# Attention and a gated feed-forward on one core: first batch's sums by a product with ones, weights summed as integers

## The chip, the cores and the metric

The kernel runs on one core of a Trainium2 chip. The metric is the device time of one execution in microseconds. Three runs of the kernel before took 865.38, 866.71 and 871.32 us; their median is 866.71 us. The engines are named as in the profile: PE multiplies matrices, PEld is its loading of weights, DVE is the vector engine, ACT the scalar engine, POOL is GpSimd, and SP issues most transfers. L502 is line 502 of the kernel before.

## The reference

The reference computes attention with a threshold, for 8 batches of 8 heads with 576 tokens of 64 numbers, and then a feed-forward over the 4608 rows of 512 numbers that come out of it.

```python
scores = scale * np.matmul(q, k.transpose(0, 1, 3, 2))
thresh = np.max(scores, axis=-1, keepdims=True) - tau
scores = np.where(scores >= thresh, scores, -1000000000.0)
scores = scores - np.max(scores, axis=-1, keepdims=True)
attn = np.exp(scores)
attn = attn / (np.sum(attn, axis=-1, keepdims=True) + 1e-09)
attn_out = np.matmul(attn, v)
# the heads of a token side by side: x is 4608 x 512
h = x @ w_in
e = np.exp(h - np.max(h, axis=-1, keepdims=True))
solu = h * (e / (np.sum(e, axis=-1, keepdims=True) + 1e-09))
mu, var = mean and variance of solu over its 1024 columns
ln = (solu - mu) / np.sqrt(var + 1e-06) * g_ln
out = ln @ w_out
```

`q`, `k` and `v` are 32-bit floats. [...]

## The kernel before, in words

**Slots and rounds.** The attention is cut into 144 slots, 18 for each batch. A slot is 128 query rows of two heads (`hp` is the pair of heads). Slots of kind 0 and 1 hold the first 512 tokens of a pair of heads in four parts; the two slots of kind 2 hold what is left of all eight heads. Two slots, r = 0 and r = 1, form a unit. The main loop runs in rounds, one slot in each, and writes out by hand the order of the work on every engine; nothing is reordered afterwards. "pv(10)" below is the product pv that round 10 issues, and likewise "scores(11)".

**What a round does**, by engine, in the order of issue:

- PE: `scores` (L480) into two PSUM tiles `s0` and `s1`, one for each head of the slot. There is one buffer for each, so the next round's scores wait until ACT has read this round's. Then a part of the feed-forward (`ff_h`, L655, in two halves h0 and h1 of 32 matmul records; `ff_o`, L760), and, where a unit is due, `attend_steps`: the product pv (L590), 72 matmul records. A unit is due three or four rounds after its second slot: pv runs in rounds 5, 7, 9, 10, 12, 15, 16 and 19 for the eight units of the first batch. PE works strictly in this order, so scores(r+1) stand behind pv(r).
- DVE: `maxes` (L502) takes the largest score of each row, for two heads. Then `blocks` (L548) transposes the slot of the round before in 32 x 32 blocks into the tile `T`, with an instruction for each head; at r = 1 three transfers on SP's queue bring `T` into the tile `wT` (L557, L559), which pv reads. Then come the weights, and in later rounds the reductions of the feed-forward (L670, L685, L700).
- ACT: `ramp` (L517) and `exps` (L526) make the weights of attention from the scores; `exps` also sums each row into `sm`, which shows in the profile as an extra instruction that reads the accumulator. `attended` copies the product from PSUM to `xh` (L622), the input of the feed-forward.
- POOL: `normalise` of the slot of the round before: add 1e-9 to the sums (L533), their inverse by a power (L534), and a product for each head (L536).

**The weights.** In rounds 0 to 15 each round also turns one of 16 pieces of the weights (128 x 512 numbers, 512 KB) into floats. Pieces 0 to 7 are `w_in`, 8 to 15 are `w_out`. `weight_load` brings a piece into `raw`. `weight_a` cuts exponent (L286 on DVE, L291 on ACT) and the mantissa's upper part (L292 on DVE) out of the upper word. `weight_b` adds the lower word to the mantissa (L306) and the sign to the exponent (L309), both on DVE with two inputs. `weight_c` multiplies the two on POOL (L319), a round later and behind that round's `normalise`. For `w_out` ACT also multiplies the exponent part by the gains (`weight_gain`, L325), and `weight_d` (L332) makes a copy with the halves of the partitions swapped, by transfers on SP's queue.

**Buffers.** Two PSUM tiles (`p0`, `p1`, handed out in turn by `take`) hold the products pv, `h_ps` and `o_ps`; a tile of pv is free after the copy L622. In rounds 0, 2 and 4 `whole_pair` uses both to transpose the q and k of a pair of heads (L345 on PE, copied out by ACT). `T` and `wT` have two buffers each; `e` of a weight piece has two, its `m` one. From round 13 on PE also transposes q and k of the second batch (L345 again), which needs their transfers (`load_one`, `load_ends`, L131 and L142).

Of the kernel before, what the change touches and what calls it, by code (L numbers as in the profile page):

```python
# [20 lines left out]
def kernel(  # L21
# [61 lines left out]
    lims = [const.tile([P, 1], F32, name=f"lim{x}") for x in range(2)]  # L83

    wide = w_in.dtype == I64
    W_UNIT = 2.0**-20 if wide else 1.0
# [159 lines left out]
    def gains():  # L246
        tag, g_ps = take("g_ps")
        nc.tensor.transpose(out=g_ps[:, 0:NC], in_=g_rows, identity=ident[0:NC, 0:NC])
        nc.vector.tensor_scalar(
            out=gs, in0=g_ps[:, 0:NC], scalar1=W_UNIT, scalar2=None, op0=ALU.mult  # L250
        )
        pairs_free.append(tag)
# [5 lines left out]
    def piece(x):  # L258
        if x < 2 * NP:
            c, hf = divmod(x, 2)  # L260
            cols = slice(512 * hf, 512 * hf + 512)
            return w_in[P * c : P * c + P, cols], w1[:, c, cols], W_UNIT
        c = x - 2 * NP
        return w_out[P * c : P * c + P], w2[:, 2 * c], gs[:, c : c + 1]
# [12 lines left out]

    def weight_a(x):
        if not wide:
            return  # L280
        d = raws[x]
        hi = d["raw"].bitcast(I32).rearrange("p (n two) -> p n two", two=2)[:, :, 1]
# [8 lines left out]
        nc.scalar.activation(out=e, in_=e, func=AF.Relu, bias=lims[x >= 2 * NP], scale=8388608.0)  # L291
        nc.vector.tensor_scalar(  # L292
            out=m, in0=hi, scalar1=0xFFFFF, scalar2=0x100000,
            op0=ALU.bitwise_and, op1=ALU.bitwise_or,
        )

    def weight_b(x):
        d = raws[x]
        _, dst, unit = piece(x)
        if not wide:  # L300
            nc.vector.tensor_scalar(out=dst, in0=d["raw"], scalar1=unit, scalar2=None, op0=ALU.mult)
            return
        words = d["raw"].bitcast(I32).rearrange("p (n two) -> p n two", two=2)
        lo, hi = words[:, :, 0], words[:, :, 1]
        e, m = d["em"]
        nc.vector.scalar_tensor_tensor(  # L306
            out=dst, in0=lo.bitcast(U32), scalar=2.0**-32, in1=m, op0=ALU.mult, op1=ALU.add
        )
# [4 lines left out]
    def weight_c(x):  # L313
        d = raws.pop(x)
        if not wide:
            return
        _, dst, _ = piece(x)
        e, _ = d["em"]
        nc.gpsimd.tensor_tensor(out=dst, in0=dst, in1=e.bitcast(F32), op=ALU.mult)  # L319
# [136 lines left out]
    live = {}  # L456

# [33 lines left out]
    def maxes(s, loose):  # L491
# [3 lines left out]
        both = small.tile([P, 2], F32, tag="both", name="both") if loose else None  # L495
        for ps in d["ps"]:
# [4 lines left out]
            w = work.tile([P, S], F32, tag="w", bufs=4, name="w")  # L501
# [19 lines left out]

    def exps(s):
        d = live[s]
        d["sm"] = sm = small.tile([P, 2], F32, tag="sm", name="sm")
# [5 lines left out]
    def normalise(s):  # L530
        d = live[s]
        sm = d["sm"]
# [7 lines left out]
    def blocks(s):  # L540
# [6 lines left out]
        for h, w in enumerate(live.pop(s)["w"]):  # L547
# [20 lines left out]
    def attend_steps(key):  # L568
# [7 lines left out]
        for e in range(2) if kind == 2 else [None]:  # L576
            for m in range(NK):
                for u in range(2):
                    d, h0 = source(b * NP + (hp if e is None else e + 2 * u))
                    for h in range(2):  # L580
# [18 lines left out]
                        yield  # L599

    def attended(key):
        b, kind, hp = key
        tag, y = units.pop(key)["y"]
        y = y.rearrange("p (u n) -> p u n", u=2)[:, :, 0:P]
        if kind == 2 or b < 2:
            y = y.rearrange("p u (r y) -> p u r y", r=2)
        else:
# [7 lines left out]
        else:  # L615
# [252 lines left out]
    with tc.manual_schedule():  # L868
# [29 lines left out]
        while True:  # L898
# [29 lines left out]
            if rnd - 1 in pieces:  # L928
                weight_gain(pieces[rnd - 1])
# [113 lines left out]
            if rnd in pieces:  # L1043
# [46 lines left out]
```

## Time and profile before

| what | value |
|---|---|
| three runs | 865.38, 866.71, 871.32 us |
| span of the profiled execution | 865.3 us |
| PE busy, over the span | 820.6 us (95%) |
| DVE, ACT, POOL busy | 682.6, 574.2, 500.2 us (79%, 66%, 58%) |
| rounds 0 to 18 (first batch and one) | begin at 10.9 us, round 19 at 118.8 us |
| DVE busy, 20 to 90 us | 67.3 of 70 us |
| PE busy, 20 to 90 us | 49.1 of 70 us |
| PE busy, 200 to 800 us | 596.8 of 600 us |

The page gives the span of the profiled execution, from its first instruction to its last, and no time of its own; the fastest run, 865.38 us, is 0.1 us longer than that span, the median 1.4 us.

A round's begin is the begin of its first L502 on DVE. In order they are (us): 10.9, 16.1, 21.4, 26.8, 31.5, 36.7, 41.4, 46.6, 51.3, 56.5, 61.2, 67.0, 71.5, 78.6, 85.1, 91.9, 100.3, 106.7, 111.1 and 118.8.

How to read the views: a line of the timeline has the start, the length in us, the engine, the line of the kernel, the operation, the tiles (out<-in), the shapes, how many instructions are merged, and in square brackets the idle time of the engine before it and what ended it. A matmul in 32-bit floats leaves two records, so a count of 72 is 36 matmul instructions. "PEclk" is the clock granted to PE, as a share of full speed.

### The profile page before, as it was taken

The numbers are of one execution on the slowest core, as the hardware profiler recorded it, in microseconds if no ns is written. First come the engines' busy times: TensorE is split into PE (matmuls) and PEld (weight loads), VectorE is DVE, ScalarE is ACT, GpSimd is POOL, SyncE is SP. The second block draws the span as 40 slices with busy tenths as digits, with TensorE's granted clock in tenths as the row PEclk, the third lists the DMA queues.
The fourth block names the chain that finished last, engine by engine and source line by source line (L and its number), as shares of the span: only waits on it lengthen the run. The fifth ranks groups of instructions, "written<-read, shape, count | busy, mean of one in ns | idle before, by whom it ended". The sixth has DMA issues, their size and how long they took to land.

```text
span 865.3 us, 36120 instructions
## 1 busy us (share of the span) xinstructions
PE 820.6 (95%) x15361; PEld 633.6 (73%) x15361; DVE 682.6 (79%) x1248; ACT 574.2 (66%) x1153; POOL 500.2 (58%) x938
## 2 busy tenths in 40 slices
PE   5667999899999999999999999999999999999997
PEld 3444667677688887777777776777799998887655
DVE  4999778878788888888788887888888888787361
ACT  5887767767767767677677776777677776775121
POOL 2888656556656656565656655565666655555120
PEclk9788899999999999999999999999999999999999
DMA  8999787988878788988878877887788877655212
GB/s 256 273 261 238 192 190 176 229 237 203 222 188 232 200 191 197 225 221 191 212 190 223 204 188 186 220 221 203 190 224 229 205 180 189 154 142 139 69 38 62
DMA packets 83712, 168.54 MB, mean 195 GB/s; under 512 B 15448, under 2 KB 45152, under 8 KB 83552
## 3 DMA queue, kind: packets, MB, share of 16 engines
q1 hardware_dynamic: 82416, 164.25, 76.2%
q8 instruction: 120, 1.97, 1.0%
q10 hardware_dynamic: 1136, 2.00, 0.7%
q14 instruction: 40, 0.33, 0.1%
HBM read 46.14 MB, written 9.44 MB: 64 GB/s over the span
## 4 chain that ended last, share of the span: by engine, by line
PE 81%; DMA 7%; ACT 4%; DVE 2%; SPq 2%; issue 2%; POOL 1%; ACTq 0%; DVEq 0%
PE o_ps L760 26%; PE h_ps L655 22%; PE s_ps L480 15%; PE pv L590 15%; PE h_ps L645 3%; DMA wT<-T 3%; ACT w L517 1%; ACT w L526 1%; DMA ends<-in_q_dram 1%; DVE w L502 1%; DMA w<-w 1%; DMA qT<-flip 1%; DMA k<-in_k_dram 1%; DVE T L548 1%; POOL w L536 1%
## 5 line engine op out<-in xcount | busy, mean ns | idle before, releaser
L760 PE MATMUL o_ps<-w,uT 64*64 64x256 f32 x4608 | 274.3, 376 | 2.4 <-DMA w<-w 1.3
L502 DVE CUSTOM_DVE_ANT_0 w<-s_ps,tau_t 128x576 f32<-128x576 f32 x280 | 200.3, 753 | 87.5 <-PE s_ps L480 57.5
L517 ACT ACTIVATE w<-s_ps,nth 128x576 f32<-128x576 f32 x280 | 197.0, 739 | 104.9 <-DVE nth L502 94.1
L760 PEld LDWEIGHTS o_ps<-w,uT 64*64 64x64 f32 x4608 | 215.3, 133 | 62.8 <-ACT xh L622 11.0
L536 POOL TENSOR_SCALAR w<-w,sm 128x576 f32<-128x576 f32 x288 | 222.2, 784 | 14.3
L655 PE MATMUL h_ps<-w,xh 64*64 64x512 f32 x1856 | 225.3, 592 | 1.1 <-issue 1.1
L548 DVE STREAM_TRANSPOSE T<-w 128x576 f32<-128x576 f32 x288 | 207.6, 755 | 19.8 <-POOL w L536 19.4
L526 ACT ACTIVATE w<-w,ntau 128x576 f32<-128x576 f32 x288 | 219.6, 767 | 0.0
L590 PEld LDWEIGHTS pv<-wT,v 64*64 64x64 f32 x5760 | 179.0, 136 | 32.4 <-issue 8.5
L480 PE MATMUL s_ps<-kT,qT 64*64 64x64 f32 (+1 forms) x2048 | 183.2, 422 | 14.0 <-ACT w L517 12.1
L590 PE MATMUL pv<-wT,v 64*64 64x128 f32 (+1 forms) x5760 | 177.7, 264 | 7.4 <-DMA wT<-T 4.7
L655 PEld LDWEIGHTS h_ps<-w,xh 64*64 64x64 f32 x1856 | 134.8, 134 | 65.4 <-issue 15.6
L533 POOL TENSOR_SCALAR sm<-sm 128x2 f32<-128x2 f32 x144 | 36.5, 253 | 202.0 <-ACT w L526 198.9
L534 POOL TENSOR_TENSOR sm<-sm,mone 128x2 f32<-128x2 f32 x144 | 109.0, 757 | 12.0
L480 PEld LDWEIGHTS s_ps<-kT,qT 64*64 64x64 f32 x2048 | 78.3, 139 | 23.4 <-ACT w L517 17.3
L622 ACT COPY xh<-pv 128x256 f32<-128x256 f32 x64 | 25.2, 394 | 81.3 <-PE pv L590 81.3
L721 ACT ACTIVATE V<-u,nb,rs 128x1024 f32<-128x1024 f32 x36 | 44.7, 1241 | 38.8 <-POOL nb L711 31.8
L747 DVE STREAM_TRANSPOSE uT<-V 128x1024 f32<-128x1024 f32 x36 | 44.2, 1226 | 16.9 <-DMA V<-u 16.8
L526 ACT ACTIVATION_READ_ACCUMULATOR w<-w,ntau 128x1 f32 x288 | 55.5, 193 | 0.0
L685 DVE TENSOR_TENSOR u<-h_ps,u 128x1024 f32<-128x1024 f32 x36 | 42.8, 1189 | 9.8 <-ACT u L679 9.8
L726 DVE TENSOR_SCALAR u<-u,rs,nb 128x1024 f32<-128x1024 f32 x36 | 35.0, 973 | 17.8 <-ACT V L721 17.7
L670 DVE TENSOR_REDUCE hm<-h_ps 128x1 f32<-128x1024 f32 x36 | 42.9, 1193 | 5.4 <-PE h_ps L645 2.7
(90 smaller groups left out, 578.0 us busy)
## 6 DMA issues: line engine op xcount, KB each, us to landing
wT<-T SPq DMA_DIRECT2D x160, 288.0 KB, 6.3
wT<-T SPq DMA_DIRECT2D x64, 576.0 KB, 5.6
V<-u SPq DMA_DIRECT2D x144, 64.0 KB, 3.4
out_dram<-ob SPq DMA_DIRECT2D x71, 128.0 KB, 2.5
q<-in_q_dram SPq DMA_DIRECT2D x24, 288.0 KB, 6.2
qT<-flip SPq DMA_DIRECT2D x48, 144.0 KB, 3.5
k<-in_k_dram SPq DMA_DIRECT2D x24, 288.0 KB, 6.4
kT<-flip SPq DMA_DIRECT2D x48, 144.0 KB, 3.8
```

The lines of the kernel that those rows point to most:

```text
L480: nc.tensor.matmul(out=ps[h][ROWS[y], ks], lhsT=lhsT, rhs=d["kT"][ROWS[h], ks], start=True, stop=True,)
L502: nc.vector.tensor_tensor_reduce(out=w, in0=ps[:, 0:S], in1=(zero if loose else tau_t).to_broadcast([P, S]), scale=1.0, scalar=BIG, op0=AL ...
L517: nc.scalar.activation(out=d["w"][x], in_=d["w"][x] if d["loose"] else d["ps"][x][:, 0:S], func=AF.Prelu, bias=d["nth"][x], scale=-1.0, al ...
L526: nc.scalar.activation(out=w, in_=w, func=AF.Exp, bias=ntau, scale=1.0, accum_out=sm[:, x : x + 1])
L534: nc.gpsimd.tensor_tensor(out=sm, in0=sm, in1=mone, op=ALU.pow)
L536: nc.gpsimd.tensor_scalar(out=w, in0=w, scalar1=sm[:, x : x + 1], scalar2=1.0, op0=ALU.mult, op1=ALU.mult)
L548: nc.vector.transpose(out=T[:, :, r, h, :], in_=w)
L590: nc.tensor.matmul(out=to, lhsT=d["v"][ROWS[u], (h0 + h - u) % 4 if b > 1 else h0 + h, m ^ 4 * u if m < 8 and b < 2 else m,], rhs=rhs, sta ...
L655: mm = nc.tensor.matmul(out=h[ROWS[y], f], lhsT=x[ROWS[r], c, ROWS[y]], rhs=w1_parts[ROWS[r], c, part ^ r], start=part == 0 and c == 0, st ...
L721: nc.scalar.activation(out=V, in_=u, func=AF.Identity, bias=nb, scale=rs)
L747: nc.vector.transpose(out=uT, in_=d["V"].rearrange("p y (m x) -> p m y x", x=32))
L760: nc.tensor.matmul(out=d["o"][ROWS[z], 512 * (r ^ other) : 512 * (r ^ other) + 256], lhsT=d["uT"][ROWS[r], m].rearrange("p y x -> p (y x)" ...
```

## The change

Only the first 16 rounds and the slots of the first batch with kind 0 and 1 are touched (16 slots, eight units), apart from one allocation: the two heads' tiles `w` of a slot become one tile, for all slots.

1. **Sums by a product.** For these slots `normalise` does nothing, and `exps` no longer sums. `attend_steps` issues, behind the 36 matmuls of pv, 36 more of the same shape with a tile of ones in the place of v. They put the sum of each query row into the other half of pv's PSUM tile. `attended` lets ACT copy the sums and add 1e-9 (into the beginning of `wT`, which pv has used up); `divided`, at the end of the round, lets DVE take the inverse and multiply pv by it on its way to `xh`. ACT's copy of pv is gone.
2. **Integer sums.** For pieces 6 to 15 of the weights, ACT turns the lower word into an integer with its rounding, DVE shifts the mantissa into place (in the same instruction that cut it before), and POOL adds the two and later the exponent with the sign as 32-bit integers, so that the sum's bits are the float. The instruction L306 on DVE is gone for these ten pieces, and POOL has two additions in the place of one product. For pieces 8 to 15 POOL then multiplies by the gains, in the place of ACT.
3. **One transpose.** Both heads of these slots are transposed by one instruction of 1152 columns in the place of two of 576.

The number of instructions that SP issues, and their order, stay the same.

```diff
+    ones = const.tile([P, 64], F32, name="ones")
+    least = const.tile([P, 1], F32, name="least")
...
+        nc.gpsimd.memset(ones, 1.0)
+        nc.gpsimd.memset(least, 1e-9)
...
+        nc.gpsimd.memset(unit, 8388608.0)
-        for l, e in zip(lims, (916, 896)):
+        for l, e in zip(lims, (916, 897)):
             nc.gpsimd.memset(l, -e * 8388608.0)
...
+    SUMS = range(6, NW)
+
     def weight_a(x):
...
+        if x in SUMS:
+            nc.scalar.activation(
+                out=piece(x)[1].bitcast(I32), in_=lo.bitcast(U32), func=AF.Relu, bias=unit,
+                scale=2.0**-29,
+            )
         nc.vector.tensor_scalar(
             out=e, in0=hi, scalar1=20, scalar2=0x7FF,
             op0=ALU.logical_shift_right, op1=ALU.bitwise_and,
         )
...
+        nc.scalar.activation(out=e, in_=e, func=AF.Relu, bias=lims[x in SUMS], scale=8388608.0)
+        if x in SUMS:
+            nc.vector.tensor_scalar(
+                out=m, in0=hi, scalar1=3, scalar2=0x7FFFF8,
+                op0=ALU.logical_shift_left, op1=ALU.bitwise_and,
+            )
+        else:
+            nc.vector.tensor_scalar(
+                out=m, in0=hi, scalar1=0xFFFFF, scalar2=0x100000,
+                op0=ALU.bitwise_and, op1=ALU.bitwise_or,
+            )
+
+    def weight_sum(x):
+        if wide and x in SUMS:
+            dst = piece(x)[1].bitcast(I32)
+            nc.gpsimd.tensor_tensor(out=dst, in0=dst, in1=raws[x]["em"][1], op=ALU.add)
...
     def weight_b(x):
...
-        nc.vector.scalar_tensor_tensor(
-            out=dst, in0=lo.bitcast(U32), scalar=2.0**-32, in1=m, op0=ALU.mult, op1=ALU.add
-        )
+        if x not in SUMS:
+            nc.vector.scalar_tensor_tensor(
+                out=dst, in0=lo.bitcast(U32), scalar=2.0**-32, in1=m, op0=ALU.mult, op1=ALU.add
+            )
...
     def weight_c(x):
...
-        nc.gpsimd.tensor_tensor(out=dst, in0=dst, in1=e.bitcast(F32), op=ALU.mult)
...
-    def weight_gain(x):
-        if wide and x >= 2 * NP:
-            e = raws[x]["em"][0].bitcast(F32)
-            nc.scalar.activation(out=e, in_=e, func=AF.Copy, scale=piece(x)[2])
+        if x not in SUMS:
+            nc.gpsimd.tensor_tensor(out=dst, in0=dst, in1=e.bitcast(F32), op=ALU.mult)
+            return
+        sums = dst.bitcast(I32)
+        nc.gpsimd.tensor_tensor(out=sums, in0=sums, in1=e, op=ALU.add)
+        if x >= 2 * NP:
+            nc.gpsimd.tensor_scalar(
+                out=dst, in0=dst, scalar1=by, scalar2=1.0, op0=ALU.mult, op1=ALU.mult
+            )
...
+        d["ww"] = ww = work.tile([P, 2, S], F32, tag="w", bufs=2, name="w")
         for ps in d["ps"]:
...
-            w = work.tile([P, S], F32, tag="w", bufs=4, name="w")
+            w = ww[:, len(d["w"])]
...
+    def folds(b, kind):
+
+        return b == 0 and kind < 2
+
     def exps(s):
         d = live[s]
+        if folds(*slots[s][:2]):
+            for w in d["w"]:
+                nc.scalar.activation(out=w, in_=w, func=AF.Exp, bias=ntau, scale=1.0)
+            return
...
     def normalise(s):
         d = live[s]
+        if folds(*slots[s][:2]):
+            return
...
+        if folds(b, kind):
+            nc.vector.transpose(
+                out=T[:, :, r].rearrange("p m h x -> p h m x"),
+                in_=d["ww"].rearrange("p h (m x) -> p h m x", x=32),
+            )
+        for h, w in enumerate(d["w"] if not folds(b, kind) else ()):
             nc.vector.transpose(out=T[:, :, r, h, :], in_=w)
...
+        for m in range(NK) if folds(b, kind) else ():
+            for u in range(2):
+                for h in range(2):
+                    nc.tensor.matmul(
+                        out=y[ROWS[h], u, P : 2 * P].rearrange("p (r g x) -> p g r x", r=2, g=2),
+                        lhsT=ones[ROWS[u]], rhs=wT[ROWS[u], :, m, :, h],
+                        start=m == 0, stop=m == NK - 1,
+                    )
+                    yield
...
+        if folds(b, kind):
+            by = u["wT"].rearrange("p g m r h x -> p (g m r h x)")[:, 0 : 2 * P]
+            by = by.rearrange("p (u n) -> p u n", u=2)
+            nc.scalar.activation(
+                out=by, in_=y[:, :, P : 2 * P], func=AF.Identity, bias=least, scale=1.0
+            )
...
+        if by is not None:
+            ended.append(lambda: divided(to, y, by, tag))
+            return
         nc.scalar.copy(out=to, in_=y)
         pairs_free.append(tag)
+
+    def divided(to, y, by, tag):
+        nc.vector.reciprocal(out=by, in_=by)
+        nc.vector.tensor_tensor(out=to, in0=y, in1=by, op=ALU.mult)
+        pairs_free.append(tag)
...
             if rnd - 1 in pieces:
                 weight_c(pieces[rnd - 1])
+            if rnd in pieces:
+                weight_sum(pieces[rnd])
...
                 if x + 1 < len(pieces):
                     weight_a(x + 1)
+            while ended:
+                ended.pop(0)()
```

More of the change, by code (lines that the diff above doesn't have):

```diff
@@ L83 @@
     lims = [const.tile([P, 1], F32, name=f"lim{x}") for x in range(2)]
+    unit = const.tile([P, 1], F32, name="unit")
     wide = w_in.dtype == I64
-    W_UNIT = 2.0**-20 if wide else 1.0
     NK = S // 64
@@ L249, in gains @@
         nc.vector.tensor_scalar(
-            out=gs, in0=g_ps[:, 0:NC], scalar1=W_UNIT, scalar2=None, op0=ALU.mult
+            out=gs, in0=g_ps[:, 0:NC], scalar1=1.0, scalar2=None, op0=ALU.mult
         )
@@ L261, in piece @@
             cols = slice(512 * hf, 512 * hf + 512)
-            return w_in[P * c : P * c + P, cols], w1[:, c, cols], W_UNIT
+            return w_in[P * c : P * c + P, cols], w1[:, c, cols], 1.0
         c = x - 2 * NP
@@ L281, in weight_a @@
         d = raws[x]
-        hi = d["raw"].bitcast(I32).rearrange("p (n two) -> p n two", two=2)[:, :, 1]
+        lo, hi = words(x)
         d["em"] = e, m = [
@@ L289, in weight_a, with words @@
         )
[L291 to L294, printed above, removed]
-        )
+        nc.scalar.activation(out=e, in_=e, func=AF.Relu, bias=lims[x in SUMS], scale=8388608.0)
[13 more added lines that the diff above has]
+            nc.gpsimd.tensor_tensor(out=dst, in0=dst, in1=raws[x]["em"][1], op=ALU.add)
+    def words(x):
+        both = raws[x]["raw"].bitcast(I32).rearrange("p (n two) -> p n two", two=2)
+        return both[:, :, 0], both[:, :, 1]
     def weight_b(x):
         d = raws[x]
-        _, dst, unit = piece(x)
+        _, dst, by = piece(x)
         if not wide:
-            nc.vector.tensor_scalar(out=dst, in0=d["raw"], scalar1=unit, scalar2=None, op0=ALU.mult)
+            nc.vector.tensor_scalar(out=dst, in0=d["raw"], scalar1=by, scalar2=None, op0=ALU.mult)
             return
-        words = d["raw"].bitcast(I32).rearrange("p (n two) -> p n two", two=2)
-        lo, hi = words[:, :, 0], words[:, :, 1]
+        lo, hi = words(x)
         e, m = d["em"]
-        nc.vector.scalar_tensor_tensor(
-            out=dst, in0=lo.bitcast(U32), scalar=2.0**-32, in1=m, op0=ALU.mult, op1=ALU.add
-        )
+        if x not in SUMS:
+            nc.vector.scalar_tensor_tensor(
+                out=dst, in0=lo.bitcast(U32), scalar=2.0**-32, in1=m, op0=ALU.mult, op1=ALU.add
+            )
         nc.vector.scalar_tensor_tensor(
@@ L316, in weight_c @@
             return
-        _, dst, _ = piece(x)
+        _, dst, by = piece(x)
         e, _ = d["em"]
-        nc.gpsimd.tensor_tensor(out=dst, in0=dst, in1=e.bitcast(F32), op=ALU.mult)
-    def weight_gain(x):
-        if wide and x >= 2 * NP:
-            e = raws[x]["em"][0].bitcast(F32)
-            nc.scalar.activation(out=e, in_=e, func=AF.Copy, scale=piece(x)[2])
+        if x not in SUMS:
[7 more added lines that the diff above has]
+            )
     def weight_d(x):
@@ L456 @@
     live = {}
+    ended = []
     def scores(s, items):
@@ L546, in blocks @@
         T = u["T"]
-        for h, w in enumerate(live.pop(s)["w"]):
+        d = live.pop(s)
+        if folds(b, kind):
[4 more added lines that the diff above has]
+        for h, w in enumerate(d["w"] if not folds(b, kind) else ()):
             nc.vector.transpose(out=T[:, :, r, h, :], in_=w)
@@ L599, in attend_steps @@
                         yield
+        for m in range(NK) if folds(b, kind) else ():
[7 more added lines that the diff above has]
+                    yield
     def attended(key):
         b, kind, hp = key
-        tag, y = units.pop(key)["y"]
-        y = y.rearrange("p (u n) -> p u n", u=2)[:, :, 0:P]
+        u = units.pop(key)
+        tag, y = u["y"]
+        y = y.rearrange("p (u n) -> p u n", u=2)
+        by = None
+        if folds(b, kind):
[4 more added lines that the diff above has]
+            )
+        y = y[:, :, 0:P]
         if kind == 2 or b < 2:
             y = y.rearrange("p u (r y) -> p u r y", r=2)
+            by = by if by is None else by.rearrange("p u (r y) -> p u r y", r=2)
         else:
@@ L927 @@
             items = []
-            if rnd - 1 in pieces:
-                weight_gain(pieces[rnd - 1])
             if more:
```

## The prediction

> **What bounds the kernel now.** I read the page's forty slices first, then the chain that ended last, then the first 120 us engine by engine. Three lines of the slices (tenths busy; the last is the clock granted to PE):
>
> ```profile
> PE   5667999899999999999999999999999999999997
> DVE  4999778878788888888788887888888888787361
> PEclk9788899999999999999999999999999999999999
> ```
>
> From slice 5 on (some 90 us) PE is full and the other engines have room. Whatever the change does there to DVE, ACT or POOL is worth nothing; what it adds to PE costs its full length. Only before that can relief pay. Three stages of 10 us (PE, PEld, DVE, ACT, POOL busy, PE's clock, share of DMA, GB/s):
>
> ```profile
> 40.00:50.00 10.00, 6.34 (x136) 3.75 (x128) 9.91 (x21) 7.78 (x16) 8.31 (x10) 1.00 1.02 262
> 80.00:90.00 10.00, 6.01 (x121) 3.80 (x124) 9.21 (x20) 7.76 (x20) 7.92 (x12) 0.53 0.98 227
> 100.00:110.00 10.00, 10.00 (x196) 7.97 (x192) 8.31 (x15) 8.06 (x20) 5.08 (x8) 1.00 0.80 203
> ```
>
> Up to 60 us DVE is the bound (9.9 of 10 us) and PE has a third free; at 100 us that is reversed. The timeline of PE shows where it turns over:
>
> ```profile
> 55.33 2.94 PE L590 MATMUL pv<-wT,v 64*64 64x128 f32 x72
> ...
> 62.40 2.80 PE L590 MATMUL pv<-wT,v 64*64 64x128 f32 x66 [0.92 <-DMA wT<-T]
> ...
> 65.01 2.23 PE L480 MATMUL s_ps<-kT,qT 64*64 64x512 f32 x12
> 66.72 3.95 PE L655 MATMUL h_ps<-w,xh 64*64 64x512 f32 x32
> 70.30 1.35 PE L480 MATMUL s_ps<-kT,qT 64*64 64x64 f32 x16
> 71.27 3.81 PE L655 MATMUL h_ps<-w,xh 64*64 64x512 f32 x32
> 74.70 2.23 PE L590 MATMUL pv<-wT,v 64*64 64x128 f32 x70
> ```
>
> From 62.4 us, when the `wT` of pv(10) lands, PE goes from pv to scores to feed-forward without a gap until 78.0 us. So the turn is at round 10, not at 90 us, and five of the eight units (rounds 10, 12, 15, 16, 19) lie behind it.
>
> **DVE, rounds 1 to 9.** A round steps by 4.68 us without waits: two L502 (1.35), two L548 (1.35), L306 (0.70), L309 (0.60), L286 and L292 (0.67), starts being a little closer than lengths. Every second round is 5.2 us, since L306 begins beside a product of POOL, and since L548 waits for POOL:
>
> ```profile
> 43.57 1.29 POOL L319 TENSOR_TENSOR w<-w,em 128x512 f32<-128x512 f32 x1
> ```
>
> ```profile
> 44.35 1.07 DVE L306 SCALAR_TENSOR_TENSOR w<-raw,em 128x512 f32<-128x512 uint32 x1
> ```
>
> L306 takes 0.65 to 0.69 us alone and ends here 0.56 after L319 does. The change frees L319 of `normalise`, so it runs earlier: minus some 0.4 in rounds 1, 2 and 4, and minus 0.2 to 0.4 of waiting for POOL in each second round. The merged transpose saves under 0.1: 1.35 for two of 576, against 1.13 for 1024 columns in L747, scaled to 1152 some 1.27. From piece 6 on L306 is gone, 0.65 to 1.0 a round. I put the begin of round 5 at 2.2 us earlier, and rounds without pv at 4.0 us.
>
> **What rounds 5 to 9 give back.** pv(5) is at half clock (72 records in 3.65 us; 2.23 at full clock). The ones product behind it is as long as pv, 2.2 to 3.65; I take 2.23, as the clock rose at 40 us. scores(6), just in time before, come later, and `divided` also stands on DVE before max(6). New on that path: ACT's copy (L622, 0.37; the copy with a bias is the same size), the inverse, and the product (L685 does 1024 columns from PSUM in 1.11; 256 make 0.3). The inverse on DVE has no row: at least 0.12 (L249, 8 columns), at most 1.23 (L670, 1024 columns); I take 0.35, a 256-column row like L386 (0.4). Round 5 so grows by 2.9 and round 6 begins 0.7 late. Rounds 6 and 8 then gain 1 each; ones(7) hides under ramp(7), ones(9) does not. Round 10 begins 0.2 early. Its `wT`, from the transpose in round 8, lands about 0.7 early, which is all that is handed on.
>
> **From round 10 on.** Five ones products at 72 records x 31 ns = 2.23 us, behind one another on PE: +11.2. To set against it: the 0.7; scores(11) at full clock, as PE then has been busy for over 4 us (2.23 to 1.2: 1.0); a wait of 0.46 for the `ends` of q at 82.7, late no more; PE's gap before round 14, 2.46, shorter by 0.3; and a wait of 1.3 at 115 us for the last swapped piece of `w_out`, whose POOL part leaves earlier against PE. Sum 11.2 - 0.7 - 1.0 - 0.5 - 0.3 - 1.3 = **+7.4 us**. DVE's savings in rounds 12 to 15 (L306, 0.65 each) go into waits for PE: max(13) must follow `divided(12)`, which follows ones(12).
>
> **Costed at nothing.** ACT loses sixteen pairs of accumulator reads (0.18 a round) and eight L325 (0.61), and gets ten conversions of the lower word (0.61): it has 2 us in 10 free. POOL loses 2.4 to 2.9 us a round; two additions at L319's 1.28 and one product with the gains (0.72, as L536) make 3.3 in a round of 4. The integer addition has no row; ends are 0.72 (a one-input L536) and 2.6 (two L319). At 2.6 POOL needs 5.9 and L292, which must not overwrite `m` before POOL has read it, waits 1 to 2 us in rounds 8 and 9. `wT` and the PSUM tile of pv are held until `divided`: in rounds 6 to 14 the next user comes over 2 us later; only o(17) uses the tile at once and waits some 0.3. SP's order does not change; what waits in it is waiting for DVE or POOL, which are earlier. The one tile for both `w` adds no wait: the same transposes on DVE free it, in order.
>
> **Two rules.** The granted clock of PE is 0.67 in 80 to 82 us and 0.50 until 94, after a gap of only 2.46 us. The Trainium skill (TensorE: Matmul & The Clock Gate, What's actually happening) gives half rate after an idle window of about 3.4 us, a free-running one: by it the gap of 2.46 would not throttle, and the busier PE would stay at full clock and win more; the row says it does not need so long, so I count one clock gain only. DVE and POOL show the collision above. The skill (SBUF — State Buffer, 🔬 SBUF: two separate sides) calls it an exclusive lock that whoever starts first keeps for the whole instruction, which speaks against more two-input work on POOL; by it each meeting would cost DVE up to one POOL instruction.
>
> **Rivals.**
>
> 1. *Not slower: the ones product warms PE and the transfers come early* (25%). Excess of the slow clock: scores(14) 2.14 for 1.2, the transposes and scores of round 15 3.7 for 2.4, h0(15) 5.05 for 3.5, together 3.8. pv(5) at full clock would save 1.4 and its ones stay at 2.23; if `wT` of round 10 lands 3 us early instead of 0.7, that is 2.3. 7.4 - 3.8 - 2.3 = +1.3, and with an inverse at 0.12 and DVE's savings of rounds 13 to 15 on the path (up to 2), -1. It decides at pv(5): begun at full clock. Against it: PE's gaps around 78 and 85 us are waits for ACT and DVE, which stay. Time 862 to 870.
> 2. *Slower still: POOL gets between DVE's instructions* (22%). At 77.5 us L286 took 0.90 instead of 0.41 while an L536 was waiting. In the change POOL's addition becomes ready exactly as L309 ends, each round, beside L286 and L292. If it goes first, DVE loses up to 0.9 a round in rounds 1 to 9, some 8 us; a slow inverse adds up to 0.85 in rounds 5, 7, 9 and 12, a slow addition 2 to 3. +10 to +20: 877 to 887. Against it: DVE's next instruction needs no wait, POOL's does.
> 3. *The relief is all on the path* (5%): the stretch to 62 us shrinks at 4.0 us a round by 6 and more, and PE's adds are hidden by its gaps: 855 to 860. PE's order, pv before the next scores, speaks against it.
>
> **How the numbers follow.** My forecast, +4 to +10, has 48%. The profiled execution, 865.3 with 0.1 around it, gives 872.8; the median of three is 1.3 above that, so 874.1. I say 873, between. 1% (8.7 us, to 858.0 and 875.4) is about what a measurement of this kernel can tell from no change. Slower by more: all of rival 2 and a quarter of the forecast, 0.35. Faster by more: rival 3 and a little, 0.06. Within 1%: 0.59. The range of 861 to 884 leaves out the ends of rivals 2 and 3.
>
> **What would show it.** L306 at 0.65 in rounds 1 to 5; round 5 begun near 34.5 us, round 6 near 42; records of the ones as long as pv's, five of them with no gap ahead from 62 us on; max(13) waiting behind DVE's inverse. The forecast is wrong if round 10's pv begins before 59 us, if PE's clock is 1.0 between 80 and 95 us, or if L286 and L292 take 0.9 and more.

## The result and the profile after

The changed kernel takes **888.97 us** (median of four runs, 887.03 to 890.66); the kernel before took 868.44 us in the four runs beside it (865.38 to 871.32). The ratio is **1.0254, 95% interval 1.0206 to 1.0302**: slower by 2.5%. The forecast was 873 us, the range 861 to 884. The profiled execution took 889.92 us with a span of 888.1 us. In e4 and e5 below, one of ten runs was over 1.5% above the fastest of its kernel, and their medians leave it out.

The page's slices of the changed kernel (tenths busy; the last line is the clock granted to PE; a slice is 22.2 us):

```profile
PE   5768698989989999999999999999999999999997
DVE  5999867878958887888888888888878887787361
PEclk9979799999999999999999999999999999999999
```

PE's fifth slice (89 to 111 us) fell from 9 to 6, with an 8 two slices on, while DVE's three slices of 9 stand where they stood. The stages of 10 us (PE, PEld, DVE, ACT, POOL busy; PE's clock; share of DMA; GB/s):

```profile
40.00:50.00 10.00, 6.45 (x140) 4.80 (x137) 9.73 (x15) 6.46 (x11) 3.00 (x3) 0.89 0.80 218
80.00:90.00 10.00, 9.12 (x200) 6.85 (x204) 8.91 (x13) 5.52 (x9) 5.40 (x5) 1.00 1.04 256
90.00:100.00 10.00, 3.63 (x64) 1.11 (x56) 9.61 (x16) 7.36 (x12) 4.98 (x6) 0.78 0.85 190
100.00:110.00 10.00, 8.70 (x146) 5.94 (x150) 8.25 (x15) 9.36 (x21) 5.99 (x11) 0.71 0.59 136
```

POOL fell from 8.3 to 3.0 us of ten at 40 us and DVE, which was to be relieved, is as full as before with fewer instructions (15 where there were 21). At 90 us PE is busy 3.6 of 10 us and DVE 9.6: the turn from DVE to PE, which the kernel before had made by 62 us, is not made here.

Where the rounds begin, in us (the profiled execution of each kernel):

| round | before | after | lost so far |
|---|---|---|---|
| 3 | 26.8 | 27.0 | 0.2 |
| 5 | 36.7 | 38.2 | 1.5 |
| 6 | 41.4 | 46.2 | 4.8 |
| 10 | 61.2 | 70.5 | 9.3 |
| 13 | 78.6 | 92.5 | 13.9 |
| 16 | 100.3 | 115.8 | 15.5 |
| 19 | 118.8 | 138.2 | 19.4 |

Two things make most of this. One concerns the building of the weights: `w_in` and `w_out` arrive as 64-bit floats, and the kernel takes each number as two 32-bit words, of which the upper holds the sign, the exponent and the upper part of the mantissa. The other is the inverse. The timeline of DVE in rounds 4 to 6, and once at 90 us (L298 and L310 or L305 are the two cuts, L286 and L292 of before; L336 sets the sign, L666 is ACT's copy of the sums, L695 the inverse, L696 the product with it):

```profile
36.45 0.41 DVE L298 TENSOR_SCALAR em<-raw 128x512 int32<-128x512 int32 x1
36.79 1.49 DVE L310 TENSOR_SCALAR em<-raw 128x512 int32<-128x512 int32 x1
...
42.36 1.50 DVE L305 TENSOR_SCALAR em<-raw 128x512 int32<-128x512 int32 x1
44.02 1.75 DVE L695 RECIPROCAL wT<-wT 128x256 f32<-128x256 f32 x1 [0.17 <-ACT wT L666]
45.88 0.42 DVE L696 TENSOR_TENSOR xh<-pv,wT 128x256 f32<-128x256 f32 x1
...
90.28 1.75 DVE L695 RECIPROCAL wT<-wT 128x256 f32<-128x256 f32 x1 [1.38 <-ACT wT L666]
```

and POOL at the same time:

```profile
36.61 1.38 POOL L347 TENSOR_TENSOR w<-w,em 128x512 f32<-128x512 f32 x1 [4.18 <-DVE em L336]
```

**The collision.** POOL has nothing to normalise and waits 4.18 us for the sign (L336). It starts its product while the first cut runs (36.45 to 36.86); the first cut keeps its 0.41 us, and the second takes 1.49 and ends at 38.28, 0.29 after POOL's product. It is so in each of rounds 0 to 13, with the float product L347 as with the integer addition L350: some 1.08 us a round.

**The inverse.** L695 takes 1.75 us, and what follows it starts 1.86 us after it. It stands between the sums and the next round's largest scores in eight rounds.

What PE waits for (its timeline; L650 is the ones product, L510 the scores, L548 ACT's ramp):

```profile
37.70 3.81 PE L637 MATMUL pv<-wT,v 64*64 64x128 f32 x72 [0.62 <-ACT qe L452]
41.30 2.18 PE L650 MATMUL pv<-wT,ones 64*64 64x128 f32 x72
43.26 1.19 PE L510 MATMUL s_ps<-kT,qT 64*64 64x64 f32 x16
47.81 0.48 PE L510 MATMUL s_ps<-kT,qT 64*64 64x64 f32 x4 [3.35 <-ACT w L548]
...
59.94 0.48 PE L510 MATMUL s_ps<-kT,qT 64*64 64x64 f32 x4 [4.04 <-ACT w L548]
```

After pv, ones and scores(6), PE stands still for 3.35 us: sums, ACT's copy, inverse, product, largest score and ramp follow one another, and only then is the PSUM tile of the scores free. The clock granted in the 2 us after each of the two gaps is 0.50, so these rounds lose PE's pace too.

### The profile page after: what moved, and what is told of

Its sections match the earlier page's. It is cut to its first block, busy times and chain, and to the rows that moved or that the text cites. A ratio compares the mean times of both kernels' runs of the same rounds, so it can differ in the third digit from the quotient of the medians.

```text
span 888.1 us, 37106 instructions
## 1 busy us (share of the span) xinstructions
PE 838.5 (94%) x15937; PEld 608.2 (68%) x15937; DVE 703.3 (79%) x1238; ACT 569.8 (64%) x1123; POOL 474.2 (53%) x895
## 4 chain that ended last, share of the span: by engine, by line
PE 85%; DVE 6%; DMA 3%; issue 3%; ACT 2%; SPq 1%; ACTq 0%; DVEq 0%
PE o_ps L834 27%; PE h_ps L729 23%; PE pv L637 15%; PE s_ps L510 15%; PE h_ps L719 3%; DMA wT<-T 1%; DVE w L533 1%; DVE wT L695 1%; DVE T L590 1%; PE pv L650 1%; DMA v<-in_v_dram 1%; ACT w L548 1%; DVE em L305 1%; SPq L611 1%; PE s_ps L374 1%
## 5 line engine op out<-in xcount | busy, mean ns | idle before, releaser
L548 ACT ACTIVATE w<-s_ps,nth 128x576 f32<-128x576 f32 x280 | 193.1, 737 | 131.1 <-DVE nth L533 115.0
L577 POOL TENSOR_SCALAR w<-w,sm 128x576 f32<-128x576 f32 x256 | 197.4, 784 | 12.7
L595 DVE STREAM_TRANSPOSE T<-w 128x576 f32<-128x576 f32 x256 | 184.2, 754 | 20.3 <-POOL w L577 17.6
L637 PEld LDWEIGHTS pv<-wT,v 64*64 64x64 f32 x5760 | 167.1, 136 | 42.1 <-issue 29.5
L565 ACT ACTIVATE w<-w,ntau 128x576 f32<-128x576 f32 x256 | 195.5, 770 | 0.0
L510 PE MATMUL s_ps<-kT,qT 64*64 64x64 f32 (+1 forms) x2048 | 173.5, 429 | 20.3 <-ACT w L548 14.1
L637 PE MATMUL pv<-wT,v 64*64 64x128 f32 (+1 forms) x5760 | 169.0, 263 | 5.3 <-DMA v<-in_v_dram 2.4
L729 PEld LDWEIGHTS h_ps<-w,xh 64*64 64x64 f32 x1856 | 105.5, 134 | 94.2 <-issue 77.4
L574 POOL TENSOR_SCALAR sm<-sm 128x2 f32<-128x2 f32 x128 | 29.1, 227 | 188.2 <-ACT w L565 185.1
L575 POOL TENSOR_TENSOR sm<-sm,mone 128x2 f32<-128x2 f32 x128 | 94.4, 737 | 10.7
L510 PEld LDWEIGHTS s_ps<-kT,qT 64*64 64x64 f32 x2048 | 67.3, 140 | 29.1 <-ACT w L548 20.1
L821 DVE STREAM_TRANSPOSE uT<-V 128x1024 f32<-128x1024 f32 x36 | 44.3, 1229 | 13.8 <-DMA V<-u 13.4
L800 DVE TENSOR_SCALAR u<-u,rs,nb 128x1024 f32<-128x1024 f32 x36 | 35.7, 992 | 18.1 <-ACT V L795 18.1
```

The lines of the kernel that those rows point to most:

```text
L510: nc.tensor.matmul(out=ps[h][ROWS[y], ks], lhsT=lhsT, rhs=d["kT"][ROWS[h], ks], start=True, stop=True,)
L548: nc.scalar.activation(out=d["w"][x], in_=d["w"][x] if d["loose"] else d["ps"][x][:, 0:S], func=AF.Prelu, bias=d["nth"][x], scale=-1.0, al ...
L565: nc.scalar.activation(out=w, in_=w, func=AF.Exp, bias=ntau, scale=1.0, accum_out=sm[:, x : x + 1])
L575: nc.gpsimd.tensor_tensor(out=sm, in0=sm, in1=mone, op=ALU.pow)
L577: nc.gpsimd.tensor_scalar(out=w, in0=w, scalar1=sm[:, x : x + 1], scalar2=1.0, op0=ALU.mult, op1=ALU.mult)
L595: nc.vector.transpose(out=T[:, :, r, h, :], in_=w)
```

## The experiments

Each kernel was timed against the kernel before on the same chip. "After" below is 888.97 us, a ratio of 1.0254. The kernels ran on different chips and at different times, and a recorded ratio is not the quotient of the two medians, so the differences below, which are of medians, can be off by 2 to 3 us (for e4 the ratio lies 3 us lower than its median does).

| kernel | what | us, median of the runs counted | ratio to before, 95% |
|---|---|---|---|
| e1_order | after, both cuts ahead of the sign | 875.57 | 1.0132 (1.0095 to 1.0170) |
| e2_noinv | after, no inverse | 874.87 | 1.0106 (1.0078 to 1.0134) |
| e3_both | both | 871.33 | 1.0039 (1.0014 to 1.0064) |
| e4_noones | e3 with a ninth of the ones product | 863.72 | 0.9926 (0.9891 to 0.9961) |
| e5_halfload | e4 with 1.5 MB less loaded | 857.67 | 0.9911 (0.9878 to 0.9943) |
| n1_nonorm | before, nothing normalised in the first batch | 869.12 | 1.0032 (1.0007 to 1.0057) |
| p1_ones | parts 1 and 3 alone | 888.88 | 1.0252 (1.0212 to 1.0292) |
| p2_ints | part 2 alone | 872.76 | 1.0067 (1.0028 to 1.0105) |
| p3_trans | part 3 alone | 864.16 | 0.9983 (0.9957 to 1.0009) |
| v1_late | before, seven pieces loaded a round later | 865.46 | 1.0009 (0.9981 to 1.0038) |
| z1_busy | p1 with products by 1.0 on POOL, one constant | 893.08 | 1.0306 (1.0228 to 1.0383) |
| z2_rowscalar | p1 with products by 1.0 on POOL, a factor for each row | 886.44 | 1.0242 (1.0190 to 1.0294) |

### Taking the two causes away

**e1_order** gives DVE's sign its place behind the cuts of the next piece, so that POOL, when the sign releases it, meets neither cut. Nothing else is changed.

```diff
                 x = pieces[rnd]
                 weight_b(x)
+                if x + 1 < len(pieces):
+                    weight_a(x + 1)
+                weight_sign(x)
...
-                if x + 1 < len(pieces):
-                    weight_a(x + 1)
```

> The changed kernel with one reordering: in each round DVE cuts the next piece's exponent and mantissa (L298, L305 or L310) before it sets the sign of this piece's exponent, so that POOL's addition no longer becomes ready just ahead of a cut. Same instructions, same results. Theory A (POOL's addition gets between DVE's two cuts; 1.50 us for 0.42 in 14 rounds): the cut is back at 0.42 us, the rounds bound by DVE are 1.1 us shorter, and the time falls by 9 to 14 us, to 875 to 880. Theory B (the loss is the ones product on PE, 11 us from round 10 on): 1 to 3 us, 886 to 889.

875.57 us, 13.4 less than after by the medians and 11.4 by the means (its ten times lie in two groups). The inverse and the second cut by group in the first 120 us (count | busy, mean ns of one | idle before):

```profile
L700 DVE RECIPROCAL wT<-wT 128x256 f32<-128x256 f32 x7 | 12.3, 1753 | 13.7 <-ACT wT L671 13.7
...
L305 DVE TENSOR_SCALAR em<-raw 128x512 int32<-128x512 int32 x10 | 4.2, 418 | 0.0
```

The second cut is back at 0.42 us, and rounds 2 to 4 step by 4.5 us, 5.6 in after (round 5 begins at 34.2). POOL's product now runs beside the largest scores, which keep their 0.75 us. The inverse is untouched.

**e2_noinv** leaves the inverse out (pv is multiplied by the sum).

```diff
     def divided(to, y, by, tag):
-        nc.vector.reciprocal(out=by, in_=by)
         nc.vector.tensor_tensor(out=to, in0=y, in1=by, op=ALU.mult)
```

> The changed kernel without the inverse of the sums: pv is multiplied by the sum itself, so this kernel leaves out the eight inverses of the first batch and its output is not the reference's. Theory A (the inverse, 1.75 us for 256 columns, stands on the path of every round with a pv): 1.8 us in each of rounds 5, 7, 9, 10, 12 at least, and in 15, 16 and 19 where PE waits for it: 9 to 14 us less, 875 to 880. Theory B (PE's ones product is the path, the inverse lies beside it): 0 to 4 us.

874.87 us, 14.1 less than after; eight inverses with their 1.86 us are 14.9.

**e3_both** has both edits.

> The reordering and the missing inverse together (again the output is not the reference's: the inverses are left out). Theory A: the two add up, 18 to 26 us less than the changed kernel, 863 to 871. The forecast on record, which had neither cost, says 873 to 876, since the ones product still takes 11 us on PE.

871.33 us: 17.6 less than after, not the sum of 27.5. In the profiles, the lead that e3 has over e2 by the removed collision is 5.6 us when round 9 begins (54.3 against 59.9) and gone when round 10 begins (65.7 against 65.2). DVE's timeline in round 9 of e3 shows that it then waits for the sums (L671 is ACT's copy of them):

```profile
65.22 0.42 DVE L700 TENSOR_TENSOR xh<-pv,wT 128x256 f32<-128x256 f32 x1 [6.12 <-ACT wT L671]
```

PE's clock was 0.50 from 50.5 to 60 us there, and pv(9) waited twice for its transfer into `wT` (0.95 and 0.42 us). How much each of the two took is not shown, and the 3.5 us by which the medians of e2 and e3 still differ come later: at round 19 e3 is 0.5 us ahead (125.7 against 126.2).

### What is left, and why relief is worth little

**e4_noones** is e3 with the ones product cut from nine steps to one, so that the sums are over a ninth of the row.

```diff
-        for m in range(NK) if folds(b, kind) else ():
+        for m in range(1) if folds(b, kind) else ():
...
-                        start=m == 0, stop=m == NK - 1,
+                        start=m == 0, stop=True,
```

> As the one before, and of the nine steps of each ones product eight are left out (sums over one ninth of the keys; output not the reference's). It prices the ones product itself: 8/9 of 2.2 us in each unit. If five of the eight lie on PE's path, as forecast: 9 to 10 us less than the kernel with both edits. If PE's gaps hide them: under 3 us.

863.72 us: eight ninths of the ones product are worth 7.6 us, a whole one, scaled, 8.6; 9 to 10 was expected, and the ratios (1.0039 and 0.9926) would give that. Its records are as long as pv's (72 in 2.18 to 2.23 us in after, where they follow one another). With it nearly gone the kernel is 0.3% (by the medians) to 0.7% (by the ratio) faster than before, and that is all that is left of DVE's relief. Round 9 begins at 51.9 us, 4.6 earlier than in the kernel before, but round 10 at 60.7, only 0.5 earlier. PE's timeline shows what is late:

```profile
55.19 0.69 PE L642 MATMUL pv<-wT,v 64*64 64x128 f32 x4 [3.71 <-DMA wT<-T]
```

From 10 to 60 us transfers into `wT` take 9.7 us from issue to landing in the median (5.9 in before, 5.6 in after), and the DMA share is 0.99 (0.97 in before, 0.87 in after). In e3 they take 11.2 us.

**e5_halfload** takes bytes from e4: of pieces 5 to 10 only half the rows are loaded, the other half is set to 1.0 by POOL.

```diff
-        queue.dma_start(out=raw, in_=piece(x)[0])
+        of = slice(0, P)
+        if 5 <= x <= 10:
+            of = ROWS[0]
+            nc.gpsimd.memset(raw[ROWS[1]].bitcast(F32), 1.0)
+        queue.dma_start(out=raw[of], in_=piece(x)[0][of])
```

> The kernel with reordering, no inverse and one ninth of the ones product (output not the reference's), and beside that only half of the rows of weight pieces 5 to 10 are loaded (the other half is filled by a memset on POOL): 1.5 MB less between 27 and 65 us. If the transfers are what holds rounds 9 and 10 there (wT landing 7 to 13 us after its issue), wT lands 2 us and more earlier and round 10 begins 3 us and more earlier, at 55 to 58 us in place of 60.7, and the time falls by 2 to 5 us. If it is PE or DVE, round 10 stays near 60 us and the time within 1 us.

857.67 us, 6.1 less than e4 by the medians, though the ratios to before (0.9911 and 0.9926) hardly differ and their intervals overlap, so the gain in time is not settled. In the profiles round 10 begins at 57.4 in the place of 60.7, and transfers into `wT` land in 6.2 us in the place of 9.7, although POOL's additions, late behind the added memsets, meet the first cut in rounds 6 and 7 (1.04 and 1.36 us). So the transfers do hold rounds 9 and 10 once DVE is faster.

**v1_late** asks whether the kernel before is held by them too: pieces 8 to 14 are loaded three rounds ahead in the place of four (15 was so before).

```diff
-                for y in {0: (3, 4), 11: (), 12: (15,)}.get(x, (x + 4,)):
+                for y in {0: (3, 4), 4: ()}.get(x, (x + 4,) if x < 4 else (x + 3,)):
```

> The kernel before with the pieces 8 to 15 of the weights loaded one round later each (three rounds ahead of their use in the place of four); the same work and bytes. If transfers hold round 9 and 10 in the kernel before too (its DMA share is 0.97 from 20 to 60 us), the tile wT of the first units lands earlier, round 10 moves from 61.2 to some 60 us, and the time falls by 1 to 3 us: 863 to 866. If DVE holds them (39.3 of 40 us busy there), nothing moves: 865 to 868. If a piece then comes too late for its cut, DVE waits for it and the time is 868 or more.

865.46 us, the same; round 10 begins at 61.0 (61.2 before). There DVE is full and hides it, or the shift is too small; the run doesn't tell which.

### One part at a time

**p1_ones** has the ones product, the division and the merged transpose, with the weights of before.

```diff
-    SUMS = range(6, NW)
+    SUMS = ()
...
+    def weight_gain(x):
+        if wide and x >= 2 * NP and x not in SUMS:
+            e = raws[x]["em"][0].bitcast(F32)
+            nc.scalar.activation(out=e, in_=e, func=AF.Copy, scale=piece(x)[2])
...
+            if rnd - 1 in pieces:
+                weight_gain(pieces[rnd - 1])
```

> The first and third part of the change alone: sums by the ones product, inverse on DVE and the merged transpose, with the weights built as before (L306 on DVE, one product on POOL, the gains on ACT). Theory A: all three costs of the changed kernel are here (cut at 1.50 us, inverse 1.75, ones on PE), and L306 comes back, 0.6 us in rounds 6 to 9: 889 to 893. Theory B (the integer additions are the harm): like the kernel before plus the ones product's 7 us, 872 to 876.

888.88 us: the whole loss. The second cut takes 1.5 us in rounds 0 to 7 here, as POOL's float product meets it in the same way; for the pieces of `w_out` that product waits for ACT's gains and comes later. So the integer sums, which save L306 in ten rounds, bring the collision to six more (rounds 8 to 13), and together they change nothing that the times show (888.97 and 888.88 us).

**p2_ints** has the integer sums alone.

```diff
     def folds(b, kind):
-        return b == 0 and kind < 2
+        return False
```

> The second part alone: ten pieces summed as integers on POOL, with normalise on POOL and two transposes a slot as before. Theory A (POOL then is the bound): 2.9 us of normalise, two additions of 1.28 and 0.7 for the gains are 5.5 to 6.2 us in a round that took 4.95, and DVE's second cut waits for POOL to have read the mantissas: 5 to 12 us slower than the kernel before, 872 to 879; the cut does not collide (0.42), as normalise stands ahead of the addition. Theory B (DVE's saved 0.65 us a round counts): 862 to 865.

872.76 us. Rounds 6 to 8 step by 5.7 us and round 9 by 6.4: POOL has 2.5 to 2.9 us of normalising and two additions, and is busy 10.86 of the 11.4 us from 46.5 on. In rounds 6 to 8 its second addition meets the sign and the first cut, in rounds 9 and 10 the second cut waits 1.75 us for it. That the cuts would not collide was wrong. DVE and POOL at 50 us:

```profile
49.44 1.06 DVE L336 SCALAR_TENSOR_TENSOR em<-raw,em 128x512 int32<-128x512 int32 x1
50.42 1.49 DVE L298 TENSOR_SCALAR em<-raw 128x512 int32<-128x512 int32 x1
```

```profile
49.90 1.72 POOL L318 TENSOR_TENSOR w<-w,em 128x512 int32<-128x512 int32 x1
```

Each is longer beside the other: the sign 1.06 (0.68 alone), the cut 1.49 (0.42), the addition 1.72 (1.27).

**p3_trans** has the merged transpose alone (with the one tile for both `w`).

```diff
-    SUMS = range(6, NW)
+    SUMS = ()
...
     def folds(b, kind):
-        return b == 0 and kind < 2
+        return False
...
-        if folds(b, kind):
+        merged = b == 0 and kind < 2
+        if merged:
             nc.vector.transpose(
...
-        for h, w in enumerate(d["w"] if not folds(b, kind) else ()):
+        for h, w in enumerate(d["w"] if not merged else ()):
             nc.vector.transpose(out=T[:, :, r, h, :], in_=w)
...
+            if rnd - 1 in pieces:
+                weight_gain(pieces[rnd - 1])
```

> The third part alone: the kernel before with both heads of a slot of the first batch transposed by one instruction; sums, normalise, weights as before. The merged instruction took 1.36 to 1.37 us in the changed kernel, two single ones 0.68 each with a step of 1.35. If the merging saves DVE nothing, the first head's transpose also loses its early start (before, it could run as soon as POOL had normalised that head; merged, it waits for both). Theory A (the part is worth nothing either way): 864 to 869, within 0.3% of before. Theory B (the later start counts, 0.3 to 0.7 us in rounds 1 to 9, where DVE is the bound): 869 to 873. A gain of over 2 us would speak against both.

864.16 us, a ratio whose interval holds 1. One transpose of 1152 columns takes 1.38 us, 1.30 as a step, against a step of 1.35 for two of 576. DVE waits 7.6 us for POOL in its rounds, and round 10 begins 2.3 us later than before (63.5), yet round 19 begins at 118.9, where it was 118.8: from 60 to 100 us PE's clock was 0.87 in the place of 0.79. In one profile, then, 2.3 us of lateness at round 10 was not handed on.

### Is it the freed POOL?

**n1_nonorm** takes only work away from the kernel before: nothing is normalised in the first batch's 16 slots.

```diff
     def normalise(s):
         d = live[s]
+        if slots[s][0] == 0 and slots[s][1] < 2:
+            return
```

> The kernel before with one thing taken away: POOL's normalise is left out for the 16 slots of the first batch, so those rows stay undivided and the output is not the reference's. Nothing is added anywhere. Theory A (a POOL without work before it takes the port just between DVE's two cuts): L292 grows from 0.42 to 1.50 us in the rounds with a weight piece, L306 loses its collision (1.05 to 0.65), and rounds bound by DVE are some 0.5 us longer: 2 to 6 us slower than the kernel before, although only work was removed. Theory B (the collision comes from the integer additions): L292 stays at 0.42, the waits for POOL of 0.2 to 0.4 us vanish, and the time is that of the kernel before or up to 3 us less.

869.12 us: less work, and slower by 0.3%, a ratio whose interval only just leaves out 1 (1.0007 to 1.0057). DVE and POOL in round 3 (L309 is the sign, L286 and L292 the cuts, L319 the product):

```profile
31.04 0.68 DVE L309 SCALAR_TENSOR_TENSOR em<-raw,em 128x512 int32<-128x512 int32 x1
31.64 0.41 DVE L286 TENSOR_SCALAR em<-raw 128x512 int32<-128x512 int32 x1
31.98 1.50 DVE L292 TENSOR_SCALAR em<-raw 128x512 int32<-128x512 int32 x1
```

```profile
31.80 1.39 POOL L319 TENSOR_TENSOR w<-w,em 128x512 f32<-128x512 f32 x1 [4.31 <-DVE em L309]
```

This is the picture of the changed kernel, without any part of the change but the freed POOL, in rounds 0 to 7. In the kernel before, L319 began behind `normalise`, 2 us into the round, and met L306 in every second round for 0.4 us; freed, it meets the second cut for 1.08.

**z1_busy** tries the other direction: p1 with work added on POOL, the weights of attention multiplied by 1.0.

```diff
     def normalise(s):
         d = live[s]
         if folds(*slots[s][:2]):
+            for w in d["w"]:
+                nc.gpsimd.tensor_scalar(out=w, in0=w, scalar1=1.0, scalar2=None, op0=ALU.mult)
             return
```

> Parts 1 and 3 (p1_ones, 888.88 us) with work added: POOL multiplies both heads' weights of attention by 1.0, two products per slot of the first batch at the place where it normalised before (about 0.73 us each). The result is unchanged. Theory A (a POOL that is idle and waits for the sign starts its product between DVE's two cuts, and the second cut loses 1.1 us): kept busy, POOL comes to its product later, the cut L310 falls back from 1.50 to 0.42 us in rounds 1 to 9 and the kernel gets faster by added work: 874 to 884, against it goes that the transposes then wait for POOL (7.6 us in all of p3_trans's rounds). Rival (the collision has another cause, such as the changed buffers or the merged tile): the cut stays at 1.5 and the time at 888 or, with the wait for POOL, more.

893.08 us, and it tells nothing apart. With one constant factor the product is another instruction than in `normalise`:

```profile
36.87 3.56 POOL L578 TENSOR_SCALAR w<-w 128x576 f32<-128x576 f32 x2 [1.01 <-ACT w L566]
```

Two take 3.56 us, 1.8 each, where L536 of before takes 0.78 in the mean; and beside them the sign and the cuts take 1.15, 0.80 and 0.87 us, 1.3 more than alone.

**z2_rowscalar** repeats it with the form of `normalise`, a factor for each row and a second one.

```diff
+                nc.gpsimd.tensor_scalar(
+                    out=w, in0=w, scalar1=ones[:, 0:1], scalar2=1.0, op0=ALU.mult, op1=ALU.mult
+                )
```

> As z1_busy, with the two added products in the form that normalise has: a factor of 1.0 for each row from a tile, and a second one as a constant (in z1_busy the product with one constant took 1.81 us each, not 0.73, and stretched DVE's L336, L298 and L310 to 1.15, 0.80 and 0.87, so it kept POOL busy but was itself a second cause). If the product comes beside the cuts because POOL is idle when the sign ends, then with 1.5 us of such products ahead of it the cut L310 falls back to 0.42 us in rounds 1 to 9, round 4 begins near 31.5 as in the kernel before (33.4 in p1_ones, 33.8 in z1_busy), and the kernel is faster than p1_ones by added work: 872 to 884. Rival (POOL's product meets DVE wherever it is put, or the cause lies in the changed buffers): 886 to 895 and L310, or another of DVE's instructions with one per round, longer by about 1 us.

DVE and POOL in round 3 (its L310 is the second cut):

```profile
29.58 0.89 DVE L298 TENSOR_SCALAR em<-raw 128x512 int32<-128x512 int32 x1
30.39 0.41 DVE L310 TENSOR_SCALAR em<-raw 128x512 int32<-128x512 int32 x1
30.72 0.74 DVE L538 CUSTOM_DVE_ANT_0 w<-s_ps,tau_t 128x576 f32<-128x576 f32 x1
```

```profile
28.72 2.60 POOL L578 TENSOR_SCALAR w<-w,ones 128x576 f32<-128x576 f32 x2 [1.20 <-ACT w L566]
31.30 1.26 POOL L347 TENSOR_TENSOR w<-w,em 128x512 f32<-128x512 f32 x1
```

POOL's product now comes behind the cuts and beside the largest scores, which keep their 0.74 us. The second cut is at 0.41, the first at 0.89, as an added product meets it: rounds 2 to 4 step by 5.0 us against 5.6 in p1, and round 5 begins 3.3 us earlier (35.7 against 39.0, of which 0.7 was there when round 0 began) with more work done. So, with n1, POOL's being idle when the sign ends is the cause of the second cut's 1.08 us; busy POOL still costs the first cut 0.48. The time of 886.44 us was missed (872 to 884 expected). It lies in the rival's 886 to 895 and is not told from p1's, whose interval overlaps; what tells the two theories apart is the cut, not the time. pv(5) still ran at a low clock (72 records in 3.9 us), the inverse still follows it, and at round 10 it is 3.0 us ahead of p1, at round 19 2.0.

**e1_again** is e1_order once more, since its ten times lay in two groups.

> The same kernel as e1_order once more, for a profile: its ten times lie in two groups (seven from 873 to 877, three from 882 to 885 us), and the profiled one was of the upper group. If the profile falls in the lower group, its rounds show where the two part; expected round 10 near 65 and round 19 near 127 us in the place of 67.9 and 133.3. Both cuts stay at 0.42 us in either group.

878.03 us, a single run, between the two groups (873 to 877 and 882 to 885). Round 6 begins at 41.8 against 43.6, and what differs just ahead of it is pv(5). In PE's timeline of the first profile of e1:

```profile
34.75 4.19 PE L642 MATMUL pv<-wT,v 64*64 64x128 f32 x72 [0.62 <-ACT qe L457]
```

and of the second:

```profile
34.80 2.26 PE L642 MATMUL pv<-wT,v 64*64 64x128 f32 x71 [1.62 <-ACT qe L457]
```

The granted clock from 34.8 to 38 us was 0.50 in the one and 1.00 in the other, at the same place in the same kernel. At round 10 and at round 19 the second is 1.4 us ahead (66.5 and 131.9 against 67.9 and 133.3), less than the expected 65 and 127; the rest of the 6.5 us between the spans (876.2 and 882.7) comes in later rounds, and its cause was not looked for.

## Why the prediction was wrong

**Rival 2 was what happened; it had 22%, and the forecast of 48% costed its cause as a gain.** The forecast said of `normalise` that "the change frees L319 of `normalise`, so it runs earlier", worth 0.4 us in rounds 1, 2 and 4. L306 did fall to 0.66 us. But the freed product went to the second cut. Rival 2 named the place (the cuts L286 and L292, as the sign ends) and a price of up to 0.9 us a round in rounds 1 to 9; it was 1.08 in rounds 0 to 13, on the second cut alone, and the time of 888.97 us passed even that rival's 877 to 887. What was held against it, that DVE's next instruction needs no wait and POOL's does, is true of the first cut and not of the second: POOL's wait is over while the first cut runs. The row at 77.5 us that the rival rested on (a cut of 0.90 us) was the better evidence, though it was read wrongly: the L536 beside it was not waiting but running, from 76.6 to 78.1 us (1.46 us where 0.78 is the mean), and the cut ended 0.29 us after it, as in the changed kernel.

**The inverse was mis-sized.** I took 0.35 us and bounded it by 1.23, from a reduction of 1024 columns. It takes 1.75, 1.86 as a step. The bound was none: a row of another operation at a larger size bounds nothing if the operation's time for a column is unknown. The inverse takes 6.8 ns a column (1.75 us over 256), L696, the product beside it, 1.6. 1.5 us more in eight rounds is +12 us from this term alone, if all of it is on the path, and leaving the inverse out gained 14.1.

**The ones product was right in its length; its price is only roughly confirmed.** 2.23 us each was forecast, 2.18 to 2.23 measured. The forecast's +7.4 is what five gains left of 11.2. Its nearest match is e3, where the collision and the inverse are gone: 871.33 us, 4.6 more than before. e4 prices the product alone, with no gain set against it, at 7.6 to 8.6 us of the 11.2. The five gains were not measured one by one.

**DVE's steps were right where nothing collides.** Round 5 was put at 34.5 us: it begins at 34.2 in e1 and 38.2 in after. Round 6 was put at 42: 43.6 and 41.8 in the two profiles of e1, 46.2 in after. That the second of e1 fits is partly luck, as its inverse is 1.5 us longer than the forecast's; e3, without an inverse, begins round 6 at 39.8.

**The relief's worth came out near, by luck, as its limit was not seen.** I let only 0.7 us of DVE's relief come through to round 10, as pv and ones eat it up. With no inverse, no collision and hardly any ones product it is still 0.5 us at round 10 (e4), as the transfers come late. That the DMA share was 0.97 stood in the profile of before.

**Costed at nothing:** POOL's integer additions take 1.27 and 1.32 us in the mean (the second beside the cut) against the 1.28 taken, and its product with the gains 0.74 against 0.72. In after POOL has room. In p2, where it still normalises, it is the bound at 5.7 us a round, a case that the forecast of the whole change had no need of. The merged transpose, put at a saving of under 0.1 us, saves 0.05.

**Marks.** L306 at 0.65: so. Ones as long as pv: so. Five of them without a gap from 62 us on: not so (PE is idle 6.4 of 10 us from 90). A waiting max(13): so, the inverse at 90.28 us comes first. Of the three signs of a wrong forecast, the cut at 0.9 and more came (1.49), and the clock of 1.00 from 80 to 95 us came, without the gain that rival 1 tied to it. The Trainium skill's rule on the port (SBUF — State Buffer, 🔬 SBUF: two separate sides), quoted against the change in the prediction, agrees with the row at 36.79: the cut ends 0.29 us after POOL's product, and a meeting cost 1.08 us of that product's 1.38.

## What to carry to other kernels

Before work is taken off an engine whose instructions lengthen those of the bound one, ask what its next instruction then waits for and which instruction of the bound engine runs at that moment: an engine set free waits for the semaphore and gets in between two instructions of the other, and one changed order (the sign behind the cuts) was worth 11 to 13 us. An operation that has no row in the trace gets its price from a measurement, or its range has no upper end; and a relief is worth at most the distance to the next resource that is nearly full, here the transfers at 0.97.

## What the runs showed of the hardware

- DVE's inverse of 128x256 floats takes 1.75 us; the product of the same shape from PSUM 0.42.
- A POOL instruction with two inputs, waiting for DVE, gets in between two cuts of DVE that need no wait: 0.41, then 1.49 us. A cut that met a POOL instruction ended 0.29 us after it in five kernels (in before at 77.5 us, in after at 36.8, in n1 at 32.0, in p2 at 50.4 and in z2 at 29.6). An addition of integers on POOL takes as long as a product of floats (1.27 us for 128x512, 1.28).
- On POOL a product of 128x576 by one constant takes 1.8 us, by a factor for each row and a second factor 0.78 (1.3 beside DVE's sign and cuts in z2), and the long form also stretches DVE's sign and cuts.
- The clock of PE at one place of one kernel was 0.50 in one execution and 1.00 in another (4.19 and 2.26 us for pv(5)). After idle gaps of 3.35 and 4.04 us in after it was 0.50 in the next 2 us.
- From 10 to 60 us, transfers into `wT` that took 5.9 us to land in the median with a DMA share of 0.97 took 9.7 at 0.99 (e4), 11.2 at 0.98 (e3) and 6.2 at 0.93 (e5).
